# When w_in is converted to float32: steps 6 to 30 and pinned, in place of steps 0 to 18

## The chip, the cores and the metric

The kernel runs on one core of one Trainium2 chip. The metric is the device time of one execution in microseconds (us); a run's number is the median of its timed executions. The engines are PE (TensorE), DVE (VectorE), ACT (ScalarE), POOL (GpSimd) and SP (SyncE, which only issues transfers here).

## What is computed

Three layers in a row; x is the token array of 2304 rows by 512.

```
scores = q @ k.T / 8 + bias[head, i, j]        # 4 batches, 8 heads, 576 positions, 64 wide
attn   = softmax(scores);  x = attn @ v        # x: (2304, 512)
h = x @ w_in;  x = max(0.01 h, h) @ w_out      # w_in (512, 2048), w_out (2048, 512), given as 64-bit floats
x = gate * (relu(x @ w1[e]) @ w2[e])           # e: the expert of each token, out of 8
```

The bias is a small function of the two positions, computed on the chip. w_in and w_out arrive as 64-bit floats and are turned into 32-bit ones by integer operations on DVE.

## The kernel before

**Stages.** Ahead of the first step come 16 of the 36 bias units: DVE and ACT make relu tiles (mk), PE multiplies them (psb), ACT or DVE scales the result (bt), and it goes out to DRAM. Then 80 attention steps follow. A step is one block of up to 128 rows of two heads: PE computes scores (pss) two steps ahead, DVE adds the bias and takes the row minimum (prob, the custom instruction of L423), ACT takes the exponent (L431), DVE inverts the sums (L440, L441), POOL (in batch 0) scales the rows (L449), PE transposes (pst, psx), ACT or DVE copies, and at a group's end PE multiplies with v (psv) and DVE splits the result into a high and a low part (the tiles x). Steps 0 to 7 are batch 0's first half (256 tokens), 8 to 19 its second half (320 tokens), 20 to 27 batch 1's first half, 28 to 39 its second, and so on. The other 20 bias units are spread over steps 0 to 7.

**Up blocks.** A half's hidden layer is x @ w_in in 16 blocks of 128 columns (f = 0 to 15). One block is 12 matmuls of 256 or 320 columns into psh (w high by x high, w high by x low, w low by x high, for four parts of the 512), a copy on ACT into hst and a store to DRAM. A filler hands these blocks out between the steps' matmuls by a quota of nanoseconds for each step, oldest half first. Blocks are made as program text by a generator; which instructions an engine gets in which order is then settled by a list scheduler, which may bring an instruction forward if what it needs is there, and every engine executes its list in order.

**w_in.** Block f of w_in is loaded (w_raw, 512 KB), converted by three DVE words (L101, L105, L109, into w_t), and split into a high part (L80 on DVE for f below 8, L72 on ACT above) and a low part (L84 on DVE), both tiles wi. The jobs are spread over half-steps. Before, f's words are placed in step 2 + f (3 + f from f = 8 on), its load four half-steps (LEAD) ahead, with four w_raw buffers. The scheduler may run these words earlier than placed.

**After the steps** the remaining up blocks, the second matrix (w_out, converted by the same words in steps 35 and on), the routing and the experts follow.

Of the kernel before, what the change touches and what calls it, by code (L numbers as in the profile page):

```python
# [8 lines left out]
F32R = mybir.dt.float32r  # L9
# [3 lines left out]
U32 = mybir.dt.uint32  # L13
# [9 lines left out]
DM = 512  # L23
FF = 2048
KD = DM // 128
KF = FF // 128
# [28 lines left out]

PROBS = 4

LEAD = 4

LEAKY = (2 * S + 256) // 128  # L60

# [61 lines left out]

def w_in_split(nc, e, f):

    raw = e.cv.tile([128, KD * 256], U32, tag="w_raw", name="w_raw", bufs=4)
    src = e.w_in.rearrange("(k p) n -> p k n", p=128)
    nc.sync.dma_start(out=raw.rearrange("p (k n) -> p k n", k=KD), in_=src[:, :, 256 * f:256 * f + 256])
    yield from [None] * LEAD
    t = e.cv.tile([128, KD * 128], F32, tag="w_t", name="w_t", bufs=2)  # L130
    yield from convert_f64(nc, raw, t)
    yield
    hi, lo = w_in_columns(e, f)
    t = t.rearrange("p (k n) -> p k n", k=KD)
    COPY[WIN_HI[f // 4]](nc, hi, t)
    LO[WIN_LO[f // 4]](nc, lo, t, hi)


def host_constants():
# [378 lines left out]
def up_units(nc, e, b, hf, xh, xl):  # L518

    n = HALVES[hf][1]  # L520
    t0 = b * S + HALVES[hf][0]
    for f in range(KF):
        hst = e.hx if e.hx and f % 2 else e.late
        st = hst.tile([128, 320], F32, tag="hst", name="hst", bufs=3)
        ps = (e.psN if e.hx and f % 2 else e.psM).tile([128, 512], F32, tag="m", name="psh")
        k = 0
        wh, wl = w_in_columns(e, f)
        for kc in range(KD):
            for w, x in ((wh, xh), (wh, xl), (wl, xh)):
                nc.tensor.matmul(  # L530
                    ps[:, :n], lhsT=w[:, kc], rhs=x[:, kc, :n],
                    start=(k == 0), stop=(k == 3 * KD - 1),
                )
                k += 1
        if t0 >= 128 * LEAKY:
            nc.scalar.activation(out=st[:, :n], in_=ps[:, :n], func=AF.Copy, scale=0.01)
            nc.vector.tensor_tensor(out=st[:, :n], in0=ps[:, :n], in1=st[:, :n], op=ALU.max)  # L537
        else:
            copy_act(nc, st[:, :n], ps[:, :n])
        nc.scalar.dma_start(out=e.h_d[:, f, t0:t0 + n], in_=st[:, :n])  # L540
        yield 12 * n / 2.4


class Filler:
# [6 lines left out]
    def add(self, units):  # L551
        self.queue.append(units)

    def run(self, ns):
        self.debt += ns
        while self.queue and self.debt > 0:
            try:
                self.debt -= next(self.queue[0]) or 0.0
            except StopIteration:
                self.queue.pop(0)  # L560
        self.debt = min(self.debt, 0.0)

    def drain(self):
        self.run(float("inf"))
        self.debt = 0.0


def phase1(ctx, tc, e):

    nc = tc.nc  # L570
    early = tc.tile_pool(name="early", bufs=1, side="left")
    e.bout = early.__enter__()
    e.late = None
    at = Attention(nc, e)
    fl = Filler()
    groups = [(b, hf, p) for b in range(B) for hf in range(2) for p in range(NP)]
    steps = [g + (ib,) for g in groups for ib in HALVES[g[1]][2]]
    ns = len(steps)
    start = {}
    for n, st in enumerate(steps):  # L580
        start.setdefault(st[:3], n)


    todo = {}

    def put(n, pos, f, *args):
        todo.setdefault((max(n, 0), pos), []).append((f, args))

    def side(n, pos):
        for f, args in todo.pop((n, pos), ()):  # L590
            f(*args)

    for k, g in enumerate(groups):
        b, hf, p = g
        n0 = start[g]
        if k >= 2:
            put(n0 - 5, 1, at.q_load, g)
            put(n0 - 4, 1, at.q_hi, g)
            put(n0 - 3, 0, at.q_lo, g)
        if hf == 1:  # L600
            put(n0 - 3, 1, at.q_split_tail, g)
        if hf == 0 and k >= 2:
            m = n0 - 4 if b == 0 else start[b - 1, 1, p] + 3
            put(m, 0, at.kv_load, b, p)
            put(m, 1, at.kv_hi, b, p)
            put(m + 1, 0, at.k_lo, b, p)
            put(m + 3, 1, at.v_load, b, p)

    def spread(n, pos, job, gap):

        k = 2 * n + pos
        put(k // 2, k % 2, lambda: spread_on(k, iter(job()), gap))

    def spread_on(k, it, gap):
        try:
            next(it)
        except StopIteration:
            return
        put((k + gap) // 2, (k + gap) % 2, spread_on, k + gap, it, gap)

    for f in range(KF):
        n = 2 + f if f < KF // 2 else 3 + f
        spread((2 * n - LEAD + 1) // 2, (1 - LEAD) % 2, lambda f=f: w_in_split(nc, e, f), 1)
    for c in range(KF):
        spread(34 + 2 * c, 0, lambda c=c: w_out_narrow(nc, e, c), 1)

    bias_setup(nc, e)
    bu = bias_units(nc, e, WIDE)
    for k in range(16):
        if k == 10:  # L630
            for g in groups[:2]:
                at.q_load(g)
                at.q_hi(g)
                at.q_lo(g)
            for p in range(2):
                at.kv_load(0, p)
                at.kv_hi(0, p)
                at.k_lo(0, p)
                at.v_load(0, p)
        next(bu)  # L640
    fl.add(bu)
    for n in range(4):
        at.load_bias(steps[n])
    loaded = 4
    for n in range(2):
        for h in range(2):
            at.scores(steps[n], h)
            at.exps(steps[n], h)
    at.normalise(steps[0])

    xs = prev = None

    def values_out():
        nonlocal prev, xs
        if prev is None:
            return
        pb, ph, pp = prev
        if pp == 0:
            pool = e.xp if ph == 0 else e.late
            xs = [pool.tile([128, KD, HALVES[ph][1]], F32R, tag=f"x{i}{ph}", name=f"x{i}", bufs=1) for i in range(2)]  # L660
        at.x_split(prev, *xs)
        if pp == NP - 1:
            fl.add(up_units(nc, e, pb, ph, *xs))
        prev = None

    for n, st in enumerate(steps):
        g = st[:3]
        b, hf, p = g
        first = start[g] == n
        last = st[3] == HALVES[hf][2][-1]  # L670

        quota = 40 * 800.0 / 6.5 if n < 8 else KF * 1600.0 / 8 if hf == 0 else (13 if b == 0 else 17) * 1280.0 / 12
        nx = steps[n + 2] if n + 2 < ns else None
        while loaded < ns and at.free:
            at.load_bias(steps[loaded])
            loaded += 1
        if first:
            at.new_group()
        at.transposes(st, 0)
        values_out()  # L680
        at.transpose_tail(st)
        if nx:
            at.scores(nx, 0)
        if n + 1 < ns:
            at.normalise(steps[n + 1])
        side(n, 0)
        fl.run(quota / 2)
        if nx:
            at.exps(nx, 0)
        if st[3] != 4:  # L690
            at.transposes(st, 1)
        if nx and nx[3] != 4:
            at.scores(nx, 1)
        side(n, 1)
        at.done(st)
        if n == 7:
            fl.drain()
        else:
            fl.run(quota / 2)
        if nx and nx[3] != 4:  # L700
            at.exps(nx, 1)
        if last:
            at.pop_group(g)
            if n == 7:
                early.__exit__(None, None, None)
                e.late = ctx.enter_context(tc.tile_pool(name="late", bufs=1, side="left"))
                e.wi.append(new_w_in(e.late))
                at.free.append(PROBS)
            at.values(g)
            prev = g  # L710
    at.x_split(prev, *xs)
    fl.add(up_units(nc, e, prev[0], prev[1], *xs))
    return fl


def w_out_narrow(nc, e, c):

    raw = e.cv.tile([128, 2 * DM], U32, tag="w_raw", name="wo_raw", bufs=4)
    r = slice(128 * c, 128 * c + 128)
    nc.sync.dma_start(out=raw, in_=e.w_out[r])  # L720
    yield from [None] * LEAD
    t = e.cv.tile([128, DM], F32, tag="w_t", name="wo_t", bufs=2)
    words = convert_f64(nc, raw, t)
    with e.tc.issue_after(e.behind):
        next(words)
    yield
    yield from words
    nc.sync.dma_start(out=e.wo_d[r], in_=t)
# [419 lines left out]
class Experts:  # L1148
# [218 lines left out]
    def finish(self, s):  # L1367

        self.weights(s, False)
        self.h_t(s, 0)  # L1370
        self.h_t(s, 1)
        self.down(s, 0)
        self.down(s, 1)
# [136 lines left out]
```

## Time and profile before

| what | us |
|---|---|
| median of 3 runs | 996.77 (995.13 to 996.99) |
| profiled execution | 993.58 |
| its span in the trace | 991.8 |
| step 0 begins (first transposes of the tail, L491) | 40.8 |
| step 8 begins | 98.4 |
| step 20 begins | 158.7 |
| step 31 begins | 227.9 |
| TensorE clock granted | full in every slice |

The span leaves 1.8 us of the profiled execution around it. The times of the steps are the starts of the L491 and L487 matmuls, one in each step. In this text stage A is 0 to 40.8 us, B is steps 0 to 7 (40.8 to 98.4), C is steps 8 to 19 (98.4 to 158.7) and D is steps 20 to 30 (158.7 to 227.9).

### The profile page before, as it was taken

Reading aid. Unit: us, or ns where it says so; the run is one execution under the profiler, and the core shown is the slowest. Engines: PE = TensorE matmul, PEld = TensorE weight load, DVE = VectorE, ACT = ScalarE, POOL = GpSimd, SP = SyncE. Lnnn points to the kernel's source line nnn. Section 1 sums busy time; section 2 is a strip of 40 time slices with the busy share of each in tenths; the row PEclk is TensorE's granted clock in tenths of the full one; section 3 lists DMA queues with packets and bytes.
Section 4 is the critical chain, followed back from the end, with each engine's and each line's share of the span. In section 5 each row is a group of like instructions: output and inputs, shape, how many; then the busy total and the mean of one; then the engine's idle time right before and its main releaser. Section 6 shows DMA issues by size and latency. Waiting matters only on the chain. (4 is left out here: it accounts for less than half of the span.)

```text
span 991.8 us, 19017 instructions
## 1 busy us (share of the span) xinstructions
PE 962.8 (97%) x6294; PEld 801.0 (81%) x6294; DVE 660.7 (67%) x1668; ACT 562.9 (57%) x1146; POOL 80.8 (8%) x85
## 2 busy tenths in 40 slices
PE   6999999999999999999999999999999999999997
PEld 2455878998899889998898888888878888888885
DVE  8999987456766898778667866579984355313313
ACT  7888787778865666656454333344462455424423
POOL 0123330000000000000000000001002111111111
PEclk9999999999999999999999999999999999999999
DMA  8988998546976788546186533436506257312510
GB/s 280 277 249 283 282 296 291 151 146 192 290 230 203 237 268 277 173 143 181 50 274 216 167 110 106 129 117 241 142 22 223 66 201 269 129 43 73 181 43 35
DMA packets 137600, 180.62 MB, mean 182 GB/s; under 512 B 19841, under 2 KB 89857, under 8 KB 137362
## 3 DMA queue, kind: packets, MB, share of 16 engines
q1 hardware_dynamic: 115554, 149.83, 48.8%
q10 hardware_dynamic: 18576, 18.97, 5.4%
q0 software_dynamic: 3360, 10.49, 3.1%
q8 instruction: 52, 0.85, 0.3%
q14 instruction: 58, 0.48, 0.2%
HBM read 196.65 MB, written 43.94 MB: 243 GB/s over the span
## 5 line engine op out<-in xcount | busy, mean ns | idle before, releaser
L530 PE MATMUL psh<-x,wi 128*128 128x256 f32 (+1 forms) x1536 | 225.2, 297 | 0.5 <-DVE hst L537 0.5
L530 PEld LDWEIGHTS psh<-x,wi 128*128 128x128 f32 x1536 | 211.0, 189 | 1.2 <-DVE hst L537 0.7
L431 ACT ACTIVATE prob<-prob,stat 128x576 f32<-128x576 f32 x144 | 111.3, 773 | 40.9 <-DVE stat L423 39.2
L423 DVE CUSTOM_DVE_ANT_0 prob<-pss,prob 128x576 f32<-128x576 f32 x144 | 108.0, 753 | 36.0 <-PE pss L418 32.1
L800 PE MATMUL psx<-woh,gh 128*128 128x512 f32 x288 | 113.1, 393 | 0.0
L800 PE MATMUL psx<-wol,gh 128*128 128x512 f32 x288 | 112.5, 391 | 0.0
L800 PE MATMUL psx<-woh,gl 128*128 128x512 f32 x288 | 112.2, 390 | 0.0
L72 ACT ACTIVATE gh<-g 128x512 fp32r<-128x512 f32 x72 | 45.2, 631 | 112.4 <-PE psx L800 94.5
L84 DVE TENSOR_TENSOR htl<-pt,hth 128x512 fp32r<-128x512 f32 x40 | 25.8, 686 | 121.3 <-ACT hth L72 121.3
L469 PE MATMUL pst<-ident,prob 128*128 128x128 f32 x576 | 87.9, 277 | 4.6 <-POOL prob L449 2.5
L469 PEld LDWEIGHTS pst<-ident,prob 128*128 128x128 f32 x576 | 65.8, 140 | 23.4 <-issue 12.7
L72 ACT ACTIVATE pth<-pst 128x512 f32<-128x512 f32 (+1 forms) x120 | 65.3, 549 | 28.3 <-PE pst L469 20.9
L418 PE MATMUL pss<-kt,qhi 128*128 128x288 f32 x256 | 80.2, 330 | 0.0
L1259 POOL DMA_INDIRECT xg<-x,gidx x22 | 23.4, 1063 | 607.9 <-DMA ws<-in_mw_dram 538.7
L418 PE MATMUL pss<-kt,qlo 128*128 128x288 f32 x256 | 72.3, 298 | 0.0
L505 PE MATMUL psv<-pth,vs 128*64 128x256 f32 (+1 forms) x512 | 70.2, 412 | 0.2 <-ACT bt L280 0.2
L817 DVE SCALAR_TENSOR_TENSOR junk<-x1s,en 128x512 bf16<-128x512 f32 x96 | 66.0, 688 | 2.0 <-DMA en<-en_d 0.9
L1290 PE MATMUL pu<-w1h,xh 128*128 128x512 f32 x160 | 64.9, 405 | 0.3 <-ACT xh L72 0.3
L1321 PE MATMUL pd<-w2h,hth 128*128 128x512 f32 x160 | 62.8, 393 | 0.7 <-ACT hth L72 0.7
L800 PEld LDWEIGHTS psx<-woh,gl 128*128 128x128 f32 x288 | 54.1, 188 | 11.1
L274 PE MATMUL psb<-mk,coef 128*32 128x79 f32 (+49 forms) x640 | 50.0, 405 | 13.4 <-DVE mk L232 8.8
L800 PEld LDWEIGHTS psx<-woh,gh 128*128 128x128 f32 x288 | 54.1, 188 | 10.9
(223 smaller groups left out, 1831.7 us busy)
## 6 DMA issues: line engine op xcount, KB each, us to landing
ws<-in_mw_dram SPq DMA_DIRECT2D x164, 512.0 KB
prob<-bias SPq DMA_DIRECT2D x64, 288.0 KB
g<-h SPq DMA_DIRECT2D x72, 256.0 KB
prob<-bias SPq DMA_DIRECT2D x64, 256.0 KB
bias<-bt SPq DMA_DIRECT2D x36, 295.5 KB
h<-hst ACTq DMA_DIRECT2D x64, 160.0 KB
w_raw<-in_w_in_dram SPq DMA_DIRECT2D x16, 512.0 KB
h<-hst ACTq DMA_DIRECT2D x64, 128.0 KB
```

What stands on the lines that cost most here:

```text
L72: nc.scalar.activation(out=out, in_=in_, func=AF.Copy)
L274: nc.tensor.matmul(ps[32 * q:32 * q + 32, :b - a], lhsT=e.coef.rearrange("p g h -> p (g h)"), rhs=x, start=True, stop=True, tile_position= ...
L418: nc.tensor.matmul(ps[:, jh, :288], lhsT=lhsT, rhs=kt[:, c0 + 288 * jh:][:, :288], start=(k == 0), stop=(k == len(ops) - 1),)
L423: nc.vector.tensor_tensor_reduce(out=prv, in0=ps[:, :, :288], in1=prv, scale=-0.125, scalar=3.0e38, op0=ALU.add, op1=ALU.min, accum_out=st ...
L431: nc.scalar.activation(out=pr[:, h], in_=pr[:, h], func=AF.Exp, bias=stat[:, 0, h:h + 1], scale=-1.0, accum_out=stat[:, 1, h:h + 1],)
L469: nc.tensor.transpose(ps[:, 128 * c:128 * c + 128], pr[:, h, 64 * h + 128 * c:][:, :128], e.ident)
L505: nc.tensor.matmul(ps[64 * h:64 * h + 64, :n], lhsT=vs[:, c, h], rhs=ph[:, h, c, :n] if c < 4 else pt[:, :n], start=(c == 0), stop=(c == 4 ...
L530: nc.tensor.matmul(ps[:, :n], lhsT=w[:, kc], rhs=x[:, kc, :n], start=(k == 0), stop=(k == 3 * KD - 1),)
L800: nc.tensor.matmul(ps, lhsT=a[:, c % 4], rhs=w[:, c], start=(k == 0), stop=(k == 3 * KF - 1))
L817: nc.vector.scalar_tensor_tensor(out=junk, in0=x1, scalar=1.0, in1=e.en[:, k], op0=ALU.mult, op1=ALU.mult, accum_out=e.dots[:, t, k:k + 1],)
L1290: nc.tensor.matmul(ps, lhsT=a[:, k], rhs=w[:, k, c], start=(i == 0), stop=(i == 3 * KD - 1))
L1321: nc.tensor.matmul(ps, lhsT=a[:, k], rhs=w[:, k], start=(k == 0 and j == 0), stop=(k == 7 and j == 2))
```

## The change

A table WIN_AT places the words of each w_in block by half-steps: 12, 15, 18, 22, 26, 30, 34, 38 for f = 0 to 7 and 40 to 57 for f = 8 to 15. LEAD is 2 for w_in and w_out, and w_raw has two buffers in place of four. The first word of each block is pinned behind the reciprocal of its step, so the scheduler can't run it earlier. An up block waits in the filler (it yields None) until its w_in block is there, and the filler then goes on to the next half in its queue; in this way w_in block f serves the oldest half that lacks it. Since one half's blocks now last into the next half's steps, the x tiles of 256 tokens have two buffers, and units that would still hold a buffer are emitted in one go ahead of its reuse. The quotas are 1280 a step in steps 8 to 19 and 3491 in 20 to 30; from step 31 on they are as before.

```diff
-LEAD = 4
+LEAD = 2
+
+WIN_AT = (12, 15, 18, 22, 26, 30, 34, 38, 40, 43, 45, 48, 50, 53, 55, 57)
...
-    raw = e.cv.tile([128, KD * 256], U32, tag="w_raw", name="w_raw", bufs=4)
+    raw = e.cv.tile([128, KD * 256], U32, tag="w_raw", name="w_raw", bufs=2)
...
-    yield from convert_f64(nc, raw, t)
+    words = convert_f64(nc, raw, t)
+    with e.tc.issue_after(e.behind):
+        next(words)
+    yield
+    yield from words
     yield
...
     LO[WIN_LO[f // 4]](nc, lo, t, hi)
+    e.wi_done = f + 1
...
     for f in range(KF):
+        while f >= e.wi_done:
+            yield None
...
+    def unit(self):
+
+        for units in list(self.queue):
+            try:
+                ns = next(units)
+            except StopIteration:
+                self.queue.remove(units)
+                continue
+            if ns is not None:
+                return ns
+        return None
...
-        n = 2 + f if f < KF // 2 else 3 + f
-        spread((2 * n - LEAD + 1) // 2, (1 - LEAD) % 2, lambda f=f: w_in_split(nc, e, f), 1)
+        k = WIN_AT[f] - LEAD
+        spread(k // 2, k % 2, lambda f=f: w_in_split(nc, e, f), 1)
...
-            pool = e.xp if ph == 0 else e.late
-            xs = [pool.tile([128, KD, HALVES[ph][1]], F32R, tag=f"x{i}{ph}", name=f"x{i}", bufs=1) for i in range(2)]
+            pool, bufs = (e.xp, 2) if ph == 0 else (e.late, 1)
+            for units in ups[:-3 if ph == 0 else -1]:
+                fl.finish(units)
+            del ups[:-3 if ph == 0 else -1]
+            xs = [pool.tile([128, KD, HALVES[ph][1]], F32R, tag=f"x{i}{ph}", name=f"x{i}", bufs=bufs) for i in range(2)]
...
-        quota = 40 * 800.0 / 6.5 if n < 8 else KF * 1600.0 / 8 if hf == 0 else (13 if b == 0 else 17) * 1280.0 / 12
+        if n < 8:
+            quota = 40 * 800.0 / 6.5
+        elif b == 0:
+            quota = 1280.0
+        elif n < 31:
+            quota = (10 * 1280.0 + KF * 1600.0) / 11
+        else:
+            quota = KF * 1600.0 / 8 if hf == 0 else 17 * 1280.0 / 12
```

Three places show how the engines' lists move. The line numbers after the change are larger (L101, L105, L109 become L103, L107, L111; L530 becomes L539).

DVE in stage A, before: words of w_in (w_t, wi) among the relu tiles (mk) of the bias units.

```order
L101 TENSOR_SCALAR w_t<-w_raw 128x512
L109 SCALAR_TENSOR_TENSOR w_t<-w_raw,w_t 128x512
L232 TENSOR_SCALAR mk<-lw,v 128x416
L105 SCALAR_TENSOR_TENSOR w_t<-w_raw,w_t 128x512
L232 TENSOR_SCALAR mk<-lw,v 128x400 x2
L232 TENSOR_SCALAR mk<-lw,v 128x384 x2
L80 CAST wi_81<-w_t 128x4x128
```

DVE at the same place after the change: relu tiles, and the parts of k (kt) and q (qlo).

```order
L239 TENSOR_SCALAR mk<-lw,v 128x416 x2
L82 CAST kt<-kraw 64x576
L82 CAST kt<-kraw 64x640
L86 TENSOR_TENSOR kt<-kraw,kt 64x576
L239 TENSOR_SCALAR mk<-lw,v 128x400 x2
L239 TENSOR_SCALAR mk<-lw,v 128x384 x2
L86 TENSOR_TENSOR kt<-kraw,kt 64x640
```

No instruction of w_in stands ahead of step 6 any more. Over the whole lists, DVE's instructions on w_t and wi number before 30 ahead of step 8, 41 in steps 8 to 19 and 1 in steps 20 to 30; after the change 8, 31 and 33.

PE in step 10, before: the third matmul of an up block (the one that reads the low part, wi_82) follows the first two at once.

```order
L418 MATMUL pss<-kt,qlo 128x288
L530 MATMUL psh<-x_855,wi_81 128x256
L530 MATMUL psh<-x_856,wi_81 128x256
L530 MATMUL psh<-x_855,wi_82 128x256
L530 MATMUL psh<-x_855,wi_81 128x256
```

PE in step 10 after the change: between them stand five products with v.

```order
L425 MATMUL pss<-kt,qtail 128x288 x8
L539 MATMUL psh<-x_851,wi_81 128x256
L539 MATMUL psh<-x_852,wi_81 128x256
L512 MATMUL psv<-pth,vs 64x320 x5
L539 MATMUL psh<-x_851,wi_82 128x256
L539 MATMUL psh<-x_851,wi_81 128x256
```

DVE at that place after the change: the high part of the block (wi_81), a step's addition of the bias (L430), and the low part (wi_82).

```order
L448 RECIPROCAL stat<-stat 128x2
L82 CAST wi_81<-w_t 128x4x128
L430 ISA prob,stat<-pss,prob 128x576
L430 ISA stat 128x1
L86 TENSOR_TENSOR wi_82<-w_t,wi_81 128x4x128
```

Five of the seven up blocks that PE's list has in steps 8 to 19 after the change (14 before) are split in this way, between the second and the third matmul.

PE in step 20, before, in the middle of the step: an up block of 256 tokens ends, transposes and scores follow, and the next one begins.

```order
L530 MATMUL psh<-x_855,wi_1458 128x256
L469 MATMUL pst<-ident,prob 128x128 x4
L418 MATMUL pss<-kt,qhi 128x288
L418 MATMUL pss<-kt,qlo 128x288
L418 MATMUL pss<-kt,qhi 128x288
L418 MATMUL pss<-kt,qlo 128x288
L530 MATMUL psh<-x_855,wi_1457 128x256
```

PE in step 20 after the change: two blocks of the later half (320 tokens) ahead of the transposes, and one of the older half (256 tokens) behind them.

```order
L539 MATMUL psh<-x_1644,wi_82 128x320
L476 MATMUL pst<-ident,prob 128x128 x4
L425 MATMUL pss<-kt,qhi 128x288
L425 MATMUL pss<-kt,qlo 128x288
L425 MATMUL pss<-kt,qhi 128x288
L425 MATMUL pss<-kt,qlo 128x288
L539 MATMUL psh<-x_851,wi_81 128x256
```

By the end of step 30 both lists hold the same up blocks (38 blocks, counted as of 256 tokens), so what the change takes out of steps 8 to 19 it has put back by then.

## Rows read from the trace of the kernel before

**Rows 1.** The page: busy time and share of each engine over the span.

```profile
PE 962.8 (97%) x6294; PEld 801.0 (81%) x6294; DVE 660.7 (67%) x1668; ACT 562.9 (57%) x1146; POOL 80.8 (8%) x85
```

**Rows 2.** Busy time by stretch: A, B, C, D, then steps 48 to 59.

```profile
core 0: us, PE busy (x) PEld busy (x) DVE busy (x) ACT busy (x) POOL busy (x), PEclk, DMA share, GB/s
0.00:40.80 40.80, 29.59 (x342) 13.10 (x342) 37.87 (x95) 32.32 (x59) 3.08 (x9) 1.00 0.89 282
40.80:98.40 57.60, 53.43 (x534) 30.94 (x534) 53.28 (x138) 50.65 (x115) 15.40 (x16) 1.00 0.88 268
98.40:158.70 60.30, 56.26 (x436) 48.18 (x437) 54.21 (x131) 47.45 (x118) 18.91 (x18) 1.00 0.92 291
158.70:227.90 69.20, 68.92 (x525) 62.36 (x524) 37.20 (x98) 51.84 (x117) 0.00 (x0) 1.00 0.59 179
...
327.20:386.50 59.30, 58.66 (x462) 51.40 (x461) 52.74 (x143) 41.37 (x92) 0.00 (x0) 1.00 0.86 274
```

**Rows 3.** Waits of PE's weight loads in stage B: us, times, longest.

```profile
PEld psb L274 <- ACT bt L280: 3.5, 8, 1.0
PEld psb L274 <- DVE bt L282: 2.5, 2, 1.8
PEld pst L469 <- POOL prob L449: 2.1, 4, 0.9
```

**Rows 4.** Waits of PE's weight loads in stage C: us, times, longest.

```profile
PEld pst L469 <- ACT pth L72: 2.1, 3, 1.1
PEld pst L469 <- POOL prob L449: 2.0, 2, 1.2
PEld psx L487 <- ACT pth L72: 1.1, 1, 1.1
```

**Rows 5.** DVE's instructions on w_t alone, busy us by stage (A to D).

```profile
core 0: us, DVE busy (x), PEclk, DMA share, GB/s
0.00:40.80 40.80, 4.88 (x9) 1.00 0.89 282
40.80:98.40 57.60, 11.39 (x21) 1.00 0.88 268
98.40:158.70 60.30, 26.53 (x42) 1.00 0.92 291
158.70:227.90 69.20, 0.68 (x1) 1.00 0.59 179
```

**Rows 6.** Busy time from 11.1 us to step 0, columns as in Rows 2.

```profile
11.10:40.80 29.70, 26.53 (x316) 11.44 (x305) 29.31 (x71) 27.81 (x53) 2.34 (x2) 1.00 0.92 288
```

**Rows 7.** PE, PEld, DVE and ACT busy on psh (up blocks) in C and D.

```profile
98.40:158.70 60.30, 23.07 (x168) 21.40 (x168) 0.00 (x0) 5.12 (x14) 1.00 0.92 291
158.70:227.90 69.20, 37.09 (x240) 34.60 (x240) 0.00 (x0) 8.40 (x20) 1.00 0.59 179
```

**Rows 8.** Instructions on wi and pss: duration ns min/median/max, first and last start.

```profile
L84 DVE TENSOR_TENSOR wi<-w_t,wi x16: 671/682/828, 38.4 to 158.8; 128x512 fp32r<-128x512 f32 x16
L72 ACT ACTIVATE wi<-w_t x8: 613/618/631, 114.6 to 157.6; 128x512 fp32r<-128x512 f32 x8
...
L423 DVE CUSTOM_DVE_ANT_0 prob<-pss,prob x144: 737/751/759, 30.2 to 487.0; 128x576 f32<-128x576 f32 x144
```

**Rows 9.** Timeline of PE in step 20: start, duration, instructions.

```profile
159.38 1.59 PE L530 MATMUL psh<-x,wi 128*128 128x256 f32 x12
160.81 0.60 PE L469 MATMUL pst<-ident,prob 128*128 128x128 f32 x4
```

**Rows 10.** The SP queue's longest waits in C and D: us, times, longest.

```profile
SPq L394 <- PE pst L469: 35.5, 13, 6.8
```

More of the change, by code (lines that the diff above doesn't have):

```diff
@@ L552, in add @@
         self.queue.append(units)
+    def unit(self):
[8 more added lines that the diff above has]
+        return None
     def run(self, ns):
         self.debt += ns
[L556 to L560, printed above, removed]
+        while self.debt > 0:
+            ns = self.unit()
+            if ns is None:
+                break
+            self.debt -= ns
         self.debt = min(self.debt, 0.0)
@@ L565, in drain, with finish @@
         self.debt = 0.0
+    def finish(self, units):
+        for _ in units:
+            assert _ is not None
+        if units in self.queue:
+            self.queue.remove(units)
 def phase1(ctx, tc, e):
@@ L621, in phase1 @@
     for f in range(KF):
-        n = 2 + f if f < KF // 2 else 3 + f
-        spread((2 * n - LEAD + 1) // 2, (1 - LEAD) % 2, lambda f=f: w_in_split(nc, e, f), 1)
+        k = WIN_AT[f] - LEAD
+        spread(k // 2, k % 2, lambda f=f: w_in_split(nc, e, f), 1)
     for c in range(KF):
         spread(34 + 2 * c, 0, lambda c=c: w_out_narrow(nc, e, c), 1)
+    e.wi_done = 0
     bias_setup(nc, e)
@@ L651, in phase1 @@
     xs = prev = None
+    ups = []
     def values_out():
@@ L658, in values_out @@
         if pp == 0:
-            pool = e.xp if ph == 0 else e.late
-            xs = [pool.tile([128, KD, HALVES[ph][1]], F32R, tag=f"x{i}{ph}", name=f"x{i}", bufs=1) for i in range(2)]
+            pool, bufs = (e.xp, 2) if ph == 0 else (e.late, 1)
[3 more added lines that the diff above has]
+            xs = [pool.tile([128, KD, HALVES[ph][1]], F32R, tag=f"x{i}{ph}", name=f"x{i}", bufs=bufs) for i in range(2)]
         at.x_split(prev, *xs)
         if pp == NP - 1:
-            fl.add(up_units(nc, e, pb, ph, *xs))
+            ups.append(up_units(nc, e, pb, ph, *xs))
+            fl.add(ups[-1])
         prev = None
@@ L716, in w_out_narrow @@
 def w_out_narrow(nc, e, c):
-    raw = e.cv.tile([128, 2 * DM], U32, tag="w_raw", name="wo_raw", bufs=4)
+    raw = e.cv.tile([128, 2 * DM], U32, tag="w_raw", name="wo_raw", bufs=2)
     r = slice(128 * c, 128 * c + 128)
```

## The prediction

> **What bounds the kernel now.** I read the page's first part first: PE is busy for 97% of the span [rows 1], so over the whole program the end comes when PE's work is done, and a change that removes no matmul can gain only where PE stands or is slowed. The second view, busy time by stretch, says where that is [rows 2]. In D PE is busy for 68.92 of 69.20 us, and the 59.30 us of steps 48 to 59 look alike (58.66): there is nothing to gain, and any matmul that is added costs its full time. In A, B and C it is different. PE is idle for 11.2 us of A, 4.17 of B and 4.04 of C, and DVE is the fullest or nearly the fullest engine: 37.87 of 40.80 us (93%), 53.28 of 57.60 (92.5%), 54.21 of 60.30 (90%). ACT is close behind in B (50.65). In D DVE has only 37.20 us of work in 69.20. The third view, PE's waits, names who is late: in B evictions on ACT (3.5 us) and on DVE (2.5) and POOL's scaling (2.1) [rows 3], in C copies on ACT (2.1 and 1.1) and POOL (2.0) [rows 4]. So the first 159 us are held by several full engines together, DVE first, and D by PE alone.
>
> **The change part by part.** It takes DVE work out of the stages where DVE is full and puts it where DVE has room; but the up blocks need what is converted, so PE work goes the same way, into the stage where PE is full. The sum is made stage by stage.
>
> *Stage A.* DVE spends 4.88 us on nine instructions of w_in there [rows 5]; after the change none is left. The bounds: nothing is gained if ACT alone sets the pace, and at most ACT's own idle time can go, since ACT's work there stays. From 11.1 us to step 0 ACT is busy for 27.81 of 29.70 us and DVE for 29.31 [rows 6]. That leaves 1.89 us. Both engines are nearly full, so I take about half: **-1.0** (0 to -1.9).
>
> *Stage B.* DVE has 21 instructions of w_in, 11.39 us or 0.54 each [rows 5]; the new list keeps 8 of them (six words and the two parts of block 0), 4.3 us. DVE falls from 53.28 to 46.2 us, and ACT (50.65) becomes the fullest but for PE. No gain if ACT held the stage already; at most 57.60 - 50.65 = 6.95 us, if ACT never stood still again. Of the waits that PE's loads have there, 4.6 us name DVE or POOL, which scales what DVE's reciprocal gives it, and 3.5 name ACT [rows 3]. I count the first as recoverable by two thirds: **-3.0** (0 to -6.95).
>
> *Stage C.* DVE's instructions of w_in go from 41 in the list (42 by time, 26.53 us, 0.63 each [rows 5]) to 31: -7.0 us, DVE 47.2. ACT loses seven copies into hst at 5.12 / 14 = 0.37 [rows 7], and eight high parts at 0.62 [rows 8], which were all in C and are now in D: 47.45 - 7.5 = 40.0. PE loses seven up blocks. One block of 256 tokens occupies PE for 1.43 us, from its first matmul at 159.38 to the next instruction's at 160.81 [rows 9], so 10.0 us go, and PE's 56.26 become 46.3. DVE stays the fullest. How full can it run? In C it stands at 90%, in B at 92.5%, and from 11.1 us to step 0 at 98.7% [rows 2, 6]. At 90% the stage takes 52.4 us (-7.9), at 98.7% 47.8 (-12.5). With less PE and ACT work beside it than before I take 94%, between these: 50.2 us, **-10.1**.
>
> *Stage D.* The seven blocks come back at 1.43 us on an engine with 0.28 us of idle time [rows 2]: **+10.0**. DVE gets 32 instructions more, at 0.63 some 20 us, and has 57.4 us in 79.2 (72%). That is covered: in steps 48 to 59 DVE is at 52.74 of 59.30 (89%) and PE is idle for only 0.64 us [rows 2]. ACT gets 7.5 us to its 51.84, and has 79.2.
>
> *What costs nothing.* The loads of w_raw have two buffers and less lead: block f's load waits for the third word of block f - 2, which is three or four half-steps ahead of block f's own first word but for the last (two half-steps, one step of some 7 us there). It stands in SP's queue, whose loads of the bias wait for PE's transposes for up to 6.8 us [rows 10]; behind it wait further loads of the bias, which the queue issues some steps ahead. If that cover were gone, DVE's word would wait, and with it everything behind it on DVE; I price it at nothing and leave up to 1 us a time for the range. From step 31 on the lists hold the same work; w_out's shorter lead I price the same way.
>
> Sum: -1.0 - 3.0 - 10.1 + 10.0 = **-4.1 us**. Against the profiled execution's 993.58 that is 989.5; that execution lies 3.2 us under the median of the runs, so in terms of the median 996.77 - 4.1 = **992.7**. A measurement of this kernel can tell about 0.2%, 2 us, from no change.
>
> **The rivals.**
>
> *PE waits behind the low part (slower).* In C, a block's third matmul reads w_in's low part, and DVE makes that behind the high part and, in the place shown, an addition of the bias: 0.75 + 0.68 = 1.4 us plus its reading of the accumulator [rows 8]. PE's list is executed in order, so whatever stands behind that matmul (products with v, transposes, scores) waits too. Before, the parts were there ahead of the blocks: none of PE's listed waits in C is for wi [rows 4]. At 1.0 us for each of the seven blocks C loses 7 of its 10.1 us, and the sum is +2.9: 999.7. It decides from 4.1 / 7 = 0.6 us a block. Against it: PE has 46 us of work in 50 there, so it can stand for some 4 us in all for nothing, and its list puts five products with v between the second and the third matmul.
>
> *ACT holds A and B, and C gives back only what D takes (same).* Then A and B give under 1 us each, C runs at the 90% that DVE has there now (-7.9) and D takes +10.0: about 0 to +1, 997. For it: ACT is at 94% from 11.1 us to step 0 [rows 6], and the first row of PE's waits in B is ACT's [rows 3].
>
> *All stalls go (faster).* With every upper bound, A -1.9, B -6.95, C -12.5, D +10.0: -11.4, 985.4. For it: each of the three stages had DVE at 90% or more. Against it: B would need an ACT that never waits. [...]
>
> **How the numbers follow.** The forecast's own case, a gain of 2 to 8 us, has 0.46; all stalls gone (over 8) 0.13; no change 0.24; slower by over 2 us, nearly all of it PE behind the low part, 0.17. So faster is 0.59, same 0.24, slower 0.17. The range runs from the upper bounds (985) to the slower rival at its 1 us a block (1000); the forecast's own range is 989 to 995.
>
> **What would show it.** By the times at which steps 0, 8, 20 and 31 begin: 39.8, 94.4, 144.6 and 223.8 by the forecast. Between steps 8 and 20 DVE's instructions on w_t should sum to some 19.6 us, and PE's waits for wi should stay under 0.6 us a block. D should be about 79 us with PE busy for over 99%, and from step 31 on the two traces should run in parallel. The forecast is wrong if step 8 comes at 97 us or later (ACT held B), if PE's loads wait for wi by more than 4 us in all in C, or if PE stands in D for the words on DVE or for a half's last blocks, which are emitted in one go when they are late.

## The result and the profile after

The changed kernel takes **1000.81 us** (median of 6 runs, 999.49 to 1004.88) against 996.17 (994.58 to 996.99) for the kernel before beside it: a ratio of 1.0051 [1.0035, 1.0067]. It is 4.6 us slower, where 4.1 us faster was forecast. (The ratio, with its 95% interval, is the record's; the quotient of the two medians would be 1.0047.) Measured twice more, with a profile each, it had 1.0075 [1.0061, 1.0089] and 1.0066 [1.0052, 1.0080].

The profiled execution of the changed kernel (1004.88 us) is its longest, and both of before (993.58, and 993.83 in a second profile) lie under before's median. So the traces differ by 9.6 us on average where the medians differ by 4.6 to 7.4, and a stage is read here from all profiles of a kernel. In two of the sets of runs below one execution of the kernel before took 1934.52 and 2457.5 us; the ratios leave it out. The table has the length of each stretch, by the starts of the L491 and L487 transposes (L498 and L494 after the change).

| stretch, us | forecast | before, two profiles | changed, three profiles | mean change |
|---|---|---|---|---|
| A, to step 0 | 39.8 | 40.8, 43.0 | 42.6, 44.1, 43.1 | +1.4 |
| B, steps 0 to 7 | 54.6 | 57.6, 56.9 | 59.9, 60.3, 59.2 | +2.6 |
| C, steps 8 to 19 | 50.2 | 60.3, 59.6 | 52.2, 51.6, 52.0 | -8.0 |
| D, steps 20 to 30 | 79.2 | 69.2, 69.3 | 80.0, 79.2, 79.2 | +10.2 |
| steps 31 to 36 | no change | 29.4, 29.3 | 29.5, 29.5, 29.5 | +0.2 |
| steps 37 to 39 | no change | 14.5, 14.6 | 18.8, 17.1, 18.2 | +3.5 |
| from step 40 to the span's end | no change | 720.0, 719.3 | 720.1, 719.2, 719.1 | -0.2 |

The changed kernel's first profile, in the order of the rows of before. The page's engine line [rows 1]: PE has the same 6294 matmuls and is busy for 10 us more.

```profile
PE 972.8 (97%) x6294; PEld 803.9 (80%) x6294; DVE 661.2 (66%) x1668; ACT 562.2 (56%) x1146; POOL 76.2 (8%) x85
```

Busy time by stretch, columns as in [rows 2]: A, B, C, D, steps 31 to 36, steps 37 to 39.

```profile
0.00:42.60 42.60, 31.10 (x334) 13.26 (x334) 33.56 (x86) 31.62 (x57) 2.44 (x9) 1.00 0.80 246
42.60:102.50 59.90, 57.51 (x548) 31.85 (x549) 47.99 (x123) 51.57 (x116) 14.27 (x16) 1.00 0.79 229
102.50:154.70 52.20, 49.16 (x350) 38.18 (x348) 48.72 (x119) 41.49 (x103) 15.88 (x18) 1.00 0.85 260
154.70:234.70 80.00, 79.13 (x609) 72.47 (x607) 53.07 (x133) 57.59 (x131) 0.00 (x0) 1.00 0.73 226
234.70:264.20 29.50, 29.09 (x233) 25.63 (x232) 21.09 (x56) 24.32 (x60) 0.00 (x0) 1.00 0.71 209
264.20:283.00 18.80, 16.15 (x117) 14.27 (x116) 12.30 (x31) 13.00 (x30) 0.00 (x0) 0.91 0.82 267
```

DVE was relieved: 33.56 us in A for 37.87, 47.99 in B for 53.28. Neither stage became shorter. In B DVE stands idle for 11.9 us where it stood for 4.3, and PE is busy for 57.51 of 59.90. What A and B lost lies ahead of step 1, which begins at 55.0, 56.8 and 54.8 us in place of 50.7 and 52.8. From there to step 8 it is 47.5 to 47.6 us, and it was 47.7 and 47.1, though DVE has 5 us less to do. Busy time of that stretch, columns as in [rows 2], before:

```profile
50.70:98.40 47.70, 44.17 (x463) 26.43 (x461) 44.53 (x112) 42.24 (x96) 13.86 (x14) 1.00 0.88 269
```

and after the change:

```profile
55.00:102.50 47.50, 46.46 (x455) 26.56 (x453) 39.26 (x98) 42.18 (x95) 12.71 (x14) 1.00 0.74 209
```

PE was busy for 93% of it and is now for 98%, with eight matmuls fewer. The instructions on w_t alone [rows 5] show the move itself, A to D:

```profile
0.00:42.60 42.60, 0.00 (x0) 1.00 0.80 246
42.60:102.50 59.90, 5.90 (x8) 1.00 0.79 229
102.50:154.70 52.20, 20.72 (x31) 1.00 0.85 260
154.70:234.70 80.00, 20.69 (x34) 1.00 0.73 226
```

The waits of PE's loads in C [rows 4] hold little for w_in's two parts (wi on DVE): 1.2 us over seven blocks; the last row is the matmuls' own list.

```profile
PEld pst L476 <- POOL prob L456: 3.4, 4, 1.3
PEld pss L425 <- DVE stat L430: 1.2, 3, 0.7
...
PEld psh L539 <- DVE wi L86: 1.0, 2, 0.5
...
PEld psh L539 <- DVE wi L82: 0.2, 1, 0.2
...
PE psh L539 <- DVE wi L86: 0.3, 1, 0.3
```

Two waits stand out that the first profile of before lacks. In stage A, DVE waits for the raw block of k (kraw, one buffer). First the waits of DVE ahead of step 1, then its timeline:

```profile
DVE bt L289 <- PE psb L281: 4.9, 4, 2.2
DVE kt L82 <- DMA kraw<-in_k_dram: 2.7, 2, 1.9
```

```profile
13.66 3.22 DVE L239 TENSOR_SCALAR mk<-lw,v 128x528 f32<-128x528 f32 x8
18.73 0.45 DVE L82 CAST kt<-kraw 64x576 fp32r<-64x576 f32 x1 [1.85 <-DMA kraw<-in_k_dram]
```

In the first profile of before kraw's load was issued at 12.60 us in place of 14.15, and the same copies ran at 16.93 without a wait, with two words of w_in among the instructions ahead of them. The second is in steps 37 to 39: ACT's copy of the next batch's kraw waits, and PE behind it. Rows of the timelines of SP, ACT and PE:

```profile
261.09 0.34 SPq L761 DMA_DIRECT2D wo_raw<-in_w_out_dram  x1
261.49 0.42 SPq L325 DMA_DIRECT2D kraw<-in_k_dram  x1
...
268.89 0.68 ACT L74 ACTIVATE kt<-kraw 64x576 fp32r<-64x576 f32 x1 [2.54 <-DMA kraw<-in_k_dram]
...
271.13 0.33 PE L498 MATMUL psx<-ident,prob 128*128 128x128 f32 x1 [2.65 <-ACT pth L74]
```

kraw's load is issued right behind that of wo_raw and its copy begins 7.4 us later. Before, it was issued at 246.84 and the copies ran at 258.78, 11.9 us later, without a wait.

### The profile page after: what moved, and what is told of

Same layout as the page of the kernel before. It is cut to its first block, busy times and chain, and to the rows that moved or that the text cites. A ratio compares the mean times of both kernels' runs of the same rounds, so it can differ in the third digit from the quotient of the medians.

```text
span 1003.1 us, 19035 instructions
## 1 busy us (share of the span) xinstructions
PE 972.8 (97%) x6294; PEld 803.9 (80%) x6294; DVE 661.2 (66%) x1668; ACT 562.2 (56%) x1146; POOL 76.2 (8%) x85
## 5 line engine op out<-in xcount | busy, mean ns | idle before, releaser
L539 PE MATMUL psh<-x,wi 128*128 128x256 f32 (+1 forms) x1536 | 226.4, 298 | 0.3 <-DVE wi L86 0.3
L539 PEld LDWEIGHTS psh<-x,wi 128*128 128x128 f32 x1536 | 211.8, 190 | 2.4 <-DVE wi L86 1.0
L430 DVE CUSTOM_DVE_ANT_0 prob<-pss,prob 128x576 f32<-128x576 f32 x144 | 107.8, 751 | 27.9 <-PE pss L425 24.6
L281 PE MATMUL psb<-mk,coef 128*32 128x79 f32 (+48 forms) x640 | 53.7, 406 | 12.1 <-DVE mk L239 10.2
L1331 PE MATMUL pu<-w1h,xl 128*128 128x512 f32 x160 | 62.9, 394 | 0.0
```

Source lines behind the costliest of these rows:

```text
L281: nc.tensor.matmul(ps[32 * q:32 * q + 32, :b - a], lhsT=e.coef.rearrange("p g h -> p (g h)"), rhs=x, start=True, stop=True, tile_position= ...
L430: nc.vector.tensor_tensor_reduce(out=prv, in0=ps[:, :, :288], in1=prv, scale=-0.125, scalar=3.0e38, op0=ALU.add, op1=ALU.min, accum_out=st ...
L539: nc.tensor.matmul(ps[:, :n], lhsT=w[:, kc], rhs=x[:, kc, :n], start=(k == 0), stop=(k == 3 * KD - 1),)
L1331: nc.tensor.matmul(ps, lhsT=a[:, k], rhs=w[:, k, c], start=(i == 0), stop=(i == 3 * KD - 1))
```

## The experiments

Each kernel was timed in five rounds beside the kernel before, but for e8, a single profiled execution. The medians of the kernel before in the four sets of kernels that were timed together: 995.09 (e1 to e4), 995.44 (e5 to e8), 995.73 (e9 to e12), 995.30 (e13 to e16).

| kernel | median, us | ratio to before | interval |
|---|---|---|---|
| e1_again, e13_changed: the change | 1002.53, 1001.71 | 1.0075, 1.0066 | 1.0061 to 1.0089, 1.0052 to 1.0080 |
| e2_pin: before and the pin | 1000.21 | 1.0056 | 1.0038 to 1.0074 |
| e4_early6: change, blocks 0 to 5 early | 1000.45 | 1.0046 | 1.0031 to 1.0061 |
| e5_lead4: change, w_out's lead 4 | 1002.41 | 1.0072 | 1.0058 to 1.0085 |
| e6_kraw2_lead4: that, two kraw buffers | 998.33 | 1.0038 | 1.0024 to 1.0053 |
| e7_before_kraw2: before, two kraw buffers | 998.48 | 1.0042 | 1.0027 to 1.0057 |
| e9_split: change, blocks 0 to 7 at old places | 998.67 | 1.0031 | 1.0021 to 1.0042 |
| e10_split_kraw2 | 999.37 | 1.0047 | 1.0029 to 1.0065 |
| e11_nopin: change without the pin | 997.33 | 1.0019 | 1.0007 to 1.0031 |
| e14_nopin_lead4: that, leads of 4 | 997.86 | 1.0028 | 1.0014 to 1.0042 |
| e12_raw2: before, buffers and lead | 999.10 | 1.0028 | 1.0008 to 1.0048 |
| e16_before_lead2: before, lead alone | 998.51 | 1.0036 | 1.0023 to 1.0049 |
| e15_before_buf2: before, buffers alone | 993.96 | **0.9984** | 0.9975 to 0.9993 |

**e1_again, e8_before_look, e13_changed.** The changed kernel, the kernel before, the changed kernel, unaltered.

> The changed kernel once more, unchanged. Its first profile lies 4 us over the median of its runs, so this shows what repeats. First theory (the engines' lists): the late starts of steps 0 and 1 (42.6 and 55.0 us, against 40.8 and 50.7 before) come again within 1 us, since they follow from the order of DVE's and SP's lists; the 2.6 us stand of PE in step 37 behind a late load of k comes again in some form, 1 to 3 us. Second theory (chance of this one execution): steps 0 and 1 start within 1.5 us of before and step 37 has no stand. Median 999.5 to 1002.5 by both.

> The kernel before once more, unchanged, for a second profile. Its first profile had 993.58 us, under its own median of 996.2, and stage A's start of step 1 at 50.7 us. Theory (the lists of the changed kernels make stage A longer): step 1 again begins within 0.8 us of 50.7. Rival (a good part of the 4.3 us to step 1 is a chance of that one execution): step 1 begins 1.5 us or more later than 50.7, and the rest of the steps follow in parallel.

The table of stretches has their stages. e1 bears out its first theory in kind: steps 0 and 1 begin late again, even 1.5 and 1.8 us later than in the first profile, and PE stands (has nothing it can run) for 2.52 us in steps 37 to 39. e8 is its rival's case. The second profile of before begins step 1 at 52.8 us in place of 50.7, and has won back 1.5 us of that by step 20: so 2 us of stage A are chance, and a stage's difference of that size from one profile says nothing. It also shows a wait for kraw, which the first one lacks (1.4 us in A).

**e2_pin.** The kernel before with the pin alone.

```diff
-    yield from convert_f64(nc, raw, t)
+    words = convert_f64(nc, raw, t)
+    with e.tc.issue_after(e.behind):
+        next(words)
+    yield
+    yield from words
```

> The kernel before, with the first word of each w_in block pinned behind the reciprocal of its step; places (steps 2 to 18), four buffers and lead as before. The seven words of stage A go into steps 2 to 4. First theory (in stage A DVE's words fill holes in a chain of relu tile, matmul and eviction, and without them the list brings parts of k ahead of the relu tiles): step 1 begins 2 to 4 us later than 50.7, median 997.5 to 1000. Second theory (DVE's throughput sets the pace of stage A): step 0 begins up to 2 us earlier, and the time is given back in steps 2 to 8; median 995 to 998.

The pin alone costs 5 us. No word is left in A here either, yet A is 41.2 us and step 1 begins at 52.1. Neither theory had where: the loss is in B, in steps 6 and 7. Step 6 begins 1.3 us after that of before's first profile and step 8 5.5 us (0.2 us before and 4.1 after those of the second). Busy time by 2 us, 94 to 102 us (columns as in [rows 2]), and PE's timeline ahead of it:

```profile
94.00:96.00 2.00, 0.83 (x7) 0.60 (x6) 2.00 (x5) 1.34 (x3) 1.59 (x2) 1.00 0.95 308
96.00:98.00 2.00, 1.51 (x12) 1.27 (x11) 1.33 (x5) 1.36 (x3) 0.82 (x1) 0.89 0.90 228
98.00:100.00 2.00, 2.00 (x9) 1.50 (x7) 2.00 (x7) 1.62 (x5) 0.41 (x1) 0.50 1.03 324
100.00:102.00 2.00, 2.00 (x12) 1.09 (x12) 2.00 (x4) 0.87 (x2) 1.57 (x2) 0.75 0.80 287
```

```profile
95.72 0.66 PE L473 MATMUL pst<-ident,prob 128*128 128x128 f32 x4 [1.17 <-POOL prob L453]
96.88 0.33 PE L495 MATMUL psx<-ident,prob 128*128 128x128 f32 x1 [0.49 <-POOL prob L453]
```

PE waits twice for POOL's scaling, 1.7 us in all, and then TensorE is granted 0.50 over 98 to 100 us and gets through 9 matmuls in these 2 us. The low clock is not the whole loss: one of e2's six executions had a mean granted clock of 0.999, where the kernel before in its set had 0.997 to 0.999, and took 999.12 us, still 4.0 over 995.09.

**e3_less.** The kernel before with one word a block in place of three. The second and third words' bits are left out, so w_in's values are others and the tokens' experts too; only the stages ahead of the routing are read, and its time (1025.88 us) is not compared.

```diff
-    yield from convert_f64(nc, raw, t)
+    yield from convert_less(nc, raw, t)
```

> The kernel before without the second and third word of each w_in block (a wrong w_in: the low bits and the sign are left out), 32 instructions or 20 us of DVE's work less ahead of step 20, nothing moved and PE's work unchanged. First theory (relief of DVE is worth little, since ACT and the chain through it hold stages A and B): step 8 begins within 1.5 us of 98.4, step 20 2 to 4 us earlier, median 992 to 996. Second theory (DVE holds A and B as the prediction had it): step 8 begins 4 us or more earlier, step 20 another 4, median 986 to 990.

Two thirds of the words are gone, and A takes 47.6 us, B 55.7 and C 56.9. Their busy time, columns as in [rows 2]:

```profile
0.00:47.60 47.60, 35.36 (x359) 14.66 (x359) 40.75 (x103) 34.09 (x61) 2.36 (x9) 1.00 0.83 256
47.60:103.30 55.70, 53.58 (x527) 31.36 (x527) 47.77 (x124) 49.98 (x114) 14.83 (x16) 1.00 0.90 273
103.30:160.20 56.90, 55.46 (x432) 47.24 (x430) 38.89 (x105) 46.95 (x117) 17.39 (x18) 1.00 0.95 299
```

Up to step 8 that is 103.3, later than before's 98.4 and 99.9: A and B together give nothing back; neither theory had step 8 that late. C, where DVE fell from 54 to 38.89 us, gave back 2.7 to 3.4, as the first theory had it.

**e4_early6.** The changed kernel with blocks 0 to 5 at half-steps 5 to 15, not pinned.

```diff
-WIN_AT = (12, 15, 18, 22, 26, 30, 34, 38, 40, 43, 45, 48, 50, 53, 55, 57)
+WIN_AT = (5, 7, 9, 11, 13, 15, 34, 38, 40, 43, 45, 48, 50, 53, 55, 57)
...
-    with e.tc.issue_after(e.behind):
+    if f < 6:
         next(words)
+    else:
+        with e.tc.issue_after(e.behind):
+            next(words)
```

> The changed kernel, but blocks 0 to 5 of w_in are converted where they were before (steps 2 to 7) and not pinned; blocks 6 to 15 stay at steps 17 to 28, pinned. First theory (the lists of stages A and B are what the change spoilt): step 8 begins at 98 to 99.5 us in place of 102.5, and the median falls by 3 to 5 us, to 996 to 998. Second theory (stages A and B were not hurt by the lists; DVE's work there costs): step 8 stays at 102 or later, and the median stays at 1000 or rises.

The words are back in A and B, and step 8 begins at 101.8 us, no later than in the changed kernel. C takes 49.9 with 35.92 of DVE:

```profile
101.80:151.70 49.90, 46.90 (x349) 38.25 (x348) 35.92 (x96) 40.91 (x103) 14.15 (x18) 1.00 0.82 244
```

Steps 37 to 39 take 18.2 here too. The median is the second theory's; it is 2.1 us under e1's, the changed kernel in the same set.

**e5_lead4 and e6_kraw2_lead4.** The changed kernel with w_out's load four half-steps ahead; then two buffers for kraw as well.

```diff
-    yield from [None] * LEAD
+    yield from [None] * 4
...
-        kr = e.raw.tile([128, S + 64], F32, tag="kraw", name="kraw")
+        kr = e.raw.tile([128, S + 64], F32, tag="kraw", name="kraw", bufs=2)
```

> The changed kernel with w_out's load placed four half-steps ahead of its words again (one number; w_in's stays at two). In the changed kernel, PE stands for 2.65 us in steps 37 to 39 for an ACT copy that waits 2.54 us for kraw, and kraw's load stands in SP's list right behind the load of wo_raw, which waits for its buffer. With the number at 4 the list has kraw's load ten rows earlier, ahead of wo_raw's. Theory (the load of kraw is held by that of wo_raw): the stand goes, the distance to the kernel before does not grow between steps 37 and 40 (it grew by 4.3 us, 2.6 in the second run), and the median is 2.5 to 4.5 us below the changed kernel's 1000.8, that is 996.3 to 998.3. Rival (the transfer itself is late because all queues are full at 266 to 272 us): the stand stays at 2 us or more and the median is within 1.5 us of 1000.8.

> As e5_lead4, and kraw (the raw k block) has two buffers in place of one. Theory (without w_in's words as filler DVE stands in stage A for the one buffer of kraw, and the bias units behind it come late): DVE's waits for kraw ahead of 50 us, 2.7 us in the changed kernel, fall under 0.5, step 1 begins 1.5 to 3.5 us earlier than the changed kernel's 55.0, and the median is 1.5 to 3.5 us under that of e5_lead4. Rival (PE, ACT and the bias units' chain hold stage A; the wait only fills a hole): the waits go, but step 1 begins within 1 us of 55.0 and the median is within 1 us of e5_lead4's. Second rival (which order the list takes decides): step 1 comes later than 56.

e5 did half of what its theory said: kraw's load is issued at 255.10, the copy at 265.73 does not wait and steps 37 to 39 take 15.0 us. But the median did not fall. In its profile D takes 80.5 us (1.3 over e13's) and steps 40 to 59 116.2 (1.6 over): what was won was given back. That the stand's removal is worth 3 us in the end is not shown. e6 is 4.1 us under e5 in the same set, more than its theory's 1.5 to 3.5: DVE's waits for kraw ahead of step 1 fall from 2.7 to 0.6 us and step 1 begins at 53.0 in place of 55.0, which is half of it. That the wait is the cause is not shown: e15 below, on the kernel before, has 1.7 us of it between 8 and 43 us, and a lower ratio than e6 (0.9984 against 1.0038).

**e7_before_kraw2.** The kernel before with two kraw buffers (the second hunk above).

> The kernel before with two buffers for kraw, nothing else. It had no wait of DVE for kraw in stage A, but PE stood 11.2 us there. Theory (a single buffer costs only where words of w_in no longer fill the hole): the median is within 1.5 us of 996.2. Rival (the order of stage A's list is what counts, and any disturbance of it costs): step 1 begins 1.5 us or more later than 50.7 and the median is 1.5 to 5 us higher.

3 us slower: the rival. Step 0 begins at 46.0 us and step 1 at 54.6. An added buffer costs here 3 us, where it brought 4.1 in e6. It did not spare the wait altogether either: from 8 us to step 0 DVE still waits for kraw, for 0.3 us (0 and 1.4 in the two profiles of before). That the order of the list ahead of step 1 decides is the likely reading, but it was not traced further; steps 40 to 59 are 1.8 us longer, too (116.5 for 114.7).

**e9_split, e10_split_kraw2.** The changed kernel with blocks 0 to 7 where they were before, unpinned, and the leads of these blocks and of w_out at four half-steps (e10: with two kraw buffers, as in e6).

```diff
-WIN_AT = (12, 15, 18, 22, 26, 30, 34, 38, 40, 43, 45, 48, 50, 53, 55, 57)
+WIN_AT = (4, 6, 8, 10, 12, 14, 16, 18, 40, 43, 45, 48, 50, 53, 55, 57)
...
-    yield from [None] * LEAD
+    yield from [None] * (4 if f < 8 else LEAD)
...
-    with e.tc.issue_after(e.behind):
+    if f < 8:
         next(words)
+    else:
+        with e.tc.issue_after(e.behind):
+            next(words)
...
-        k = WIN_AT[f] - LEAD
+        k = WIN_AT[f] - (4 if f < 8 else LEAD)
...
-    yield from [None] * LEAD
+    yield from [None] * 4
```

> The changed kernel with blocks 0 to 7 of w_in at their old half-steps (4 to 18, not pinned, load four half-steps ahead) and blocks 8 to 15 as changed (steps 20 to 28, pinned); w_out's load four half-steps ahead. Up blocks move as in the changed kernel, but DVE has 11 instructions of w_in in steps 8 to 19 in place of 30, some 12 us less. Theory (DVE holds steps 8 to 19 in the changed kernel, at 93% of 52.2 us): they take 45 to 48.5 us; steps 20 to 30 take 79 to 80.5; step 8 begins at 98 to 101; the median is 2 to 6 us under that of the kernel before. Rival (they are held by the chain through DVE, POOL, PE and ACT, or by PE, and DVE only looks full): 50 to 52.5 us as in the changed kernel; the median is within 2 us of the kernel before or above it.

> As e9_split, and two buffers for kraw, which took 4.1 us off the changed kernel (e6 against e5) and added 3 to the kernel before (e7). Theory (the buffer pays where DVE has no words of w_in to fill the hole in stage A; its list has 3 of them there against e9's 10): step 1 begins within 1 us of e9_split's, and the median within 1.5 us of it. Rival (it pays by itself in a list with two x buffers): 2 us or more under e9_split.

These two, with e4, show what DVE's relief is worth in C. Its busy time in e9, columns as in [rows 2]:

```profile
103.80:153.50 49.70, 48.04 (x363) 40.69 (x361) 36.39 (x100) 39.56 (x102) 16.38 (x18) 1.00 0.83 260
```

and in e10:

```profile
101.70:153.90 52.20, 48.80 (x367) 40.71 (x366) 37.96 (x103) 42.36 (x107) 14.85 (x18) 1.00 0.84 255
```

With 11 to 12 us less on DVE (36.39 and 37.96 us in place of 48.72) C takes 49.7 and 52.2 us in place of 51.6 to 52.2. Both have one up block more there (96 matmuls into psh for 84), 1.43 us by [rows 9]. With that taken off, and e4's 49.9 beside it, DVE's fall from 93% to 73% gives back 1 to 4 us against the changed kernel's mean of 51.9. PE is busy for 47 to 49 us in all of them. Of the two theories neither had e9's number quite (49.7, between 48.5 and 50), but the medians, 2.9 and 3.6 us above before, are the rival's. Step 8 (103.8) and D (77.6) lie outside what the theory named; the block that C has more is missing in D. e10's extra buffer brought nothing, as its theory said.

**e11_nopin, e14_nopin_lead4, e13_changed.** The changed kernel without the pin (the reverse of e2's diff); e14 with `LEAD = 4` besides.

> The changed kernel without the pin: the scheduler may run the first word of a block earlier than placed, and does (28 instructions of w_in ahead of step 8, 9 of them ahead of step 0, against 5 and 0). Theory (relief of DVE in stages A and B is worth nothing, and its words there cost nothing, as they fill holes): step 8 begins at 98 to 102.5, no later than in the changed kernel; steps 8 to 19 with ten words less on DVE take 49 to 52; the median is 1 to 4 us under the changed kernel's ratio of 1.005 to 1.0075. Rival (words in A and B cost time, as my prediction had it): step 8 comes 3 us later or more than the changed kernel's 102.5.

> The changed kernel, unaltered, beside e14 to e16, so that the part of the pin is read within one set of runs (the changed kernel had 1.0051 and 1.0075 in two others, the one without the pin 1.0019 in a third). Theory (the pin costs): a ratio to the kernel before of 1.005 to 1.008, that is 1.5 to 5 us more than the kernels without the pin. Rival (the sets differ, the pin does nothing): within 1.2 us of e14.

> The changed kernel without the pin and with both leads at 4 again; the two w_raw buffers stay. Theory (the pin costs about 3 us and the lead about as much; moving the blocks costs nothing): the median is within 1.5 us of the kernel before, or under it. Rival (the lead is worth nothing with two buffers, since the load waits for the third word of the block two earlier): the ratio is e11's, 1.0007 to 1.0031; steps 37 to 40 as e11's, 15.5 us.

Without the pin 1.0019 and 1.0028, with it 1.0066 in e14's set: 3.9 us between e13 and e14 (which has the lead of 4 besides), and 4.8 between e13 and e11, with each set's kernel before taken off. By the traces DVE has 30 instructions of w_in (w_t and wi) ahead of step 8 in e11, which begins it at 101.8, and 8 in e13, which begins it at 102.3. Of the 3.8 us between the spans of e13 and e11 2.7 are in steps 37 to 39 (18.2 and 15.5 us). The loads stand in the same order there; from kraw's issue to its copy it is 6.9 us in e13 and 5.7 in e11. e14 does not beat e11: in these lists the lead is worth nothing.

**e12_raw2, e15_before_buf2, e16_before_lead2.** The kernel before with both, the buffers alone, the lead alone.

```diff
-LEAD = 4
+LEAD = 2
...
-    raw = e.cv.tile([128, KD * 256], U32, tag="w_raw", name="w_raw", bufs=4)
+    raw = e.cv.tile([128, KD * 256], U32, tag="w_raw", name="w_raw", bufs=2)
...
-    raw = e.cv.tile([128, 2 * DM], U32, tag="w_raw", name="wo_raw", bufs=4)
+    raw = e.cv.tile([128, 2 * DM], U32, tag="w_raw", name="wo_raw", bufs=2)
```

> The kernel before with two w_raw buffers and a lead of 2 half-steps, nothing else. As predicted (costs nothing): the median is within 1.5 us of the kernel before, step 1 begins at 50 to 53.5 us, and PE has no stand over 0.5 us in steps 37 to 39, since its list has the load of kraw seven rows ahead of wo_raw's there. Rival (loads that wait for their buffers in SP's list hold the loads behind them): the median is 1.5 us or more above, and PE or DVE waits for a kraw or a bias load that stands behind a load of w_raw.

> The kernel before with two w_raw buffers, its lead of four half-steps kept. e12 (both) had 1.0028. Theory (the buffers, whose loads wait in SP's list): 1.5 to 4 us above the kernel before, and the two places where e12 lost time, steps 1 to 8 (49.5 us against 47.1) and 40 to 60 (117.0 against 114.7), are the same. Rival (the lead): within 1 us of the kernel before.

> The kernel before with a lead of two half-steps, its four buffers kept. Theory (the buffers): within 1 us of the kernel before. Rival (the lead, later loads): 1.5 to 4 us above, with DVE's words waiting for w_raw's transfers. Third (any other order of the first lists costs): 1 to 3 us above with no wait for w_raw, the loss between 0 and step 8.

e12's median is its rival's (3.4 us above), but its step 1 (53.0) and its steps 37 to 39 (14.8 us, no stand of PE) are as predicted. The lead alone costs 3.2 us (998.51 against 995.30). DVE has no listed wait for w_raw in e16; steps 0 to 7 take 61.4 us in place of 57. That is the third theory there, an order of the first lists that costs. The buffers alone, which both theories had as a loss or nothing, are 1.3 us faster by the medians, ratio 0.9984: the only kernel of this study that is faster than the kernel before. In its profile steps 8 to 19 take 56.2 us in place of 59.6 and 60.3, while step 8 begins at 103.7. Why was not followed further.

## Why the prediction was wrong

**The move itself went as costed.** D has +10.2 for the forecast's +10.0: seven up blocks on a full PE [rows 9]. In C, DVE's instructions on w_t took 20.72 us where 19.6 were expected, and PE's waits for wi came to 1.5 us in all (1.2 of its loads, 0.3 of the matmuls), 0.2 a block, far under the 0.6 from which that rival decides; it did not happen. C gave back 8.0 of the 10.1 us. DVE had 48.72 us in it, not 47.2, and ran at 93.3%, not 94%. PE's busy time there fell by 7.1 us, not by the seven blocks' 10.0. Half of the difference lies in the 80 products with v: the same ones are busy for 13.14 us where it was 11.65. The other half was not followed. Busy time of psv in C (PE, PEld, DVE, then clock and transfers), of before:

```profile
98.40:158.70 60.30, 11.65 (x80) 5.40 (x80) 3.64 (x8) 1.00 0.92 291
```

and of the changed kernel:

```profile
102.50:154.70 52.20, 13.14 (x80) 5.72 (x80) 4.15 (x9) 1.00 0.85 260
```

**The step that failed is the reading of "DVE is the fullest, so DVE holds the stage",** on which A's -1.0 and B's -3.0 rest; they came out at +1.4 and +2.6. DVE was relieved by 4.3 and 5.3 us (7.1 were forecast for B), and the time did not follow: from step 1 to step 8 nothing was won, with PE busy for 98% of that stretch, and ahead of step 1 some 4 us were lost. The experiments say the same from the other side: e3 removes words and begins step 8 later than before, e11 puts 22 instructions back into A and B and begins it no later. In C the size was nearly right, but in part by luck: PE loses there what D takes back, and e4, e9 and e10 show that taking 11 to 13 us off a DVE at 93% is worth 1 to 4, so C was not held by DVE alone. The forecast's middle rival (ACT holds A and B, C gives back what D takes) comes nearest in C and D, but not in its sum, about 0 to +1; that ACT holds B is not shown either, for it is busy for 42.18 of the 47.50 us from step 1 to step 8, and PE for 46.46. The profile had the warning: PE was at 93% in B and C [rows 2], and its idle time there, 8.2 us, was all that could be won unless PE itself had less to do. In B, where PE's work stayed, the forecast's bound of 6.95 us was larger than PE's idle time of 4.17.

**What was costed at nothing cost as much as was lost.** The lead and the pin are list edits that move no work. The prediction had the lead at nothing with up to 1 us a time for the range, and no term for the pin. The pin costs 5.1 us on the kernel before (e2) and 3.9 to 4.8 in the changed one (e13 against e14 and e11). It is the one part that costs about the same in both, and alone it is most of the 4.6 to 7.4 us that were measured. The lead costs 3.2 us on the kernel before (e16) and nothing in the changed one without the pin (e14 against e11); the buffers alone are a gain of 1.3 (e15), and lead and buffers together cost 3.4 (e12).

What the move of the words and blocks is worth by itself is not settled. Two pairs of kernels differ by it alone, that is by the places, the filler, the x buffers and the quotas, each pair within one set and with two w_raw buffers and no pin. With the lead at two half-steps the moved kernel is 1.8 us faster (e11, 997.33, against e12, 999.10; the intervals of their ratios overlap), with the lead at four it is 3.9 us slower (e14, 997.86, against e15, 993.96; they do not). So the parts do not add, and in neither pair does the move bring the forecast's 4.1.

Two places where the changed kernel stands longer were seen. One is kraw's load right behind wo_raw's, with PE's stand in steps 37 to 39 (3.5 us on average over three profiles); but e5, which has no such stand, was no faster. The other is DVE's wait for kraw's single buffer in A. e6 has next to nothing of either and keeps 3 us of the loss. By its profile A (40.4 us) is no longer than before, step 0 takes 12.6 us for 9.9, and C and D together take 1.8 us more than before; no single wait was found for that rest, and its cause stays open.

"From step 31 on the two traces should run in parallel" failed at steps 37 to 39 alone. Of the times at which steps begin (39.8, 94.4, 144.6, 223.8) the second, 102.5, was the named sign that the forecast is wrong.

## What to carry to other kernels

An engine at 93% need not be the one that holds the stage: here DVE's fall from 93% to 73% of steps 8 to 19 gave back 1 to 4 us (e4, e9, e10). Ask what the next engine's busy time and waits allow when the first is relieved, and take work off it in a trial before pricing the relief. In a kernel whose lists are set by a scheduler, an edit that moves no work (a pin, a lead, a buffer) still reorders the lists, and here such edits came to between -4 and +5 us each, as much as the move that they served. Run each alone on the kernel before, and take each out of the changed kernel too: of the pin, the lead and the kraw buffer only the pin came out alike both times.

## What the runs showed of the hardware

In the changed kernel's first profile a stand of PE was followed by some 4 us at a lower clock. After the stand of 2.65 us in steps 37 to 39 the granted clock was 0.66 over 272 to 274 us and 0.50 over 274 to 276, and 0.98 in the 2 us behind them; busy time by 2 us, columns as in [rows 2]:

```profile
270.00:272.00 2.00, 0.86 (x7) 0.87 (x8) 1.87 (x6) 1.78 (x6) 0.00 (x0) 1.00 1.00 360
272.00:274.00 2.00, 2.00 (x14) 2.00 (x13) 0.00 (x0) 1.52 (x4) 0.00 (x0) 0.66 0.38 130
274.00:276.00 2.00, 2.00 (x11) 2.00 (x11) 1.34 (x3) 1.57 (x3) 0.00 (x0) 0.50 0.60 125
276.00:278.00 2.00, 2.00 (x19) 2.00 (x18) 1.49 (x6) 1.41 (x6) 0.00 (x0) 0.98 0.68 240
```

An up block of twelve matmuls of 256 columns takes 2.34 us from 274.39 us and 1.60 from 277.64, as the timeline of PE shows:

```profile
274.39 2.34 PE L539 MATMUL psh<-x,wi 128*128 128x256 f32 x12
...
277.64 1.60 PE L539 MATMUL psh<-x,wi 128*128 128x256 f32 x12
```

The clock fell after a stand of 2.03 us in e13 as well (0.63 over 270 to 272 us, 0.52 over 272 to 274), after one of 2.05 in e4 (0.50 over 268 to 270), and after the 1.7 us in two pieces in e2 (0.50 over 98 to 100). After a stand of 2.52 us at the same place in e1 it did not (1.00 in each 2 us from 270 to 280). So it differs between executions of one kernel. PE waited for ACT's copy (pth) in the changed kernel, e1, e4 and e13, and for POOL's scaling (prob) in e2. How much of the 5 us between the changed kernel's fastest and slowest run the lower clock makes is not shown: in e1 an execution with a mean granted clock of 0.995 took 1002.03 us, and two with 0.999 took 1002.08 and 1002.53.
